# Two routed experts' sums and the gates' pace in an attention, MoE and MoE kernel on one core

## The chip, the cores and the metric

One core of a Trainium2 chip runs the whole program. Its engines are TensorE (PE, matmuls, with PEld for its weight loads), VectorE (DVE), ScalarE (ACT), GpSimd (POOL) and SyncE (SP, which issues the DMAs). Each takes its own instructions in the order in which the program issued them, and waits where a value or a buffer isn't ready. The metric is the device time of one execution in microseconds; lower is better.

## The reference

Three layers follow each other: attention with a threshold on the scores, a gated MLP, and a mixture over all eight experts. Only the last is touched:

```python
logits = x @ w_gate                       # 2304 tokens, 512 wide, 8 experts
P = np.exp(logits - logits.max())
for _ in range(8):                        # 2304 x 8 table made balanced
    P /= P.sum(1, keepdims=True) + 1e-09
    P /= P.sum(0, keepdims=True) + 1e-09
    P *= N / E
for e in range(E):                        # every expert on every token
    h = np.maximum(x @ w1[e], 0.0)        # 512 -> 1024
    out += P[:, e:e + 1] * (h @ w2[e])    # 1024 -> 512
```

## The kernel before

**Number format.** Every fp32 product is three matmuls: each operand is split into a high part (a copy by ACT in a shorter format) and a low part (the rest, one subtraction on POOL or DVE), and high x high, high x low and low x high are added in PSUM (`mm3`, lines 844 to 846, and `up`, lines 1207 to 1209).

**Passes and steps.** The 2304 tokens go through the experts in three passes `u` of 768 tokens, two blocks of 384. A pass has 32 steps: eight experts, four pairs of 128-wide slices of the inner width each (`PAIRS` = 4, `NG` = 32). The steps are numbered `k` = 0 to 95; `g = k % NG` is a step's number in its pass and `g // PAIRS` its expert.

**A step.** `up(k, u)` makes the hidden values of four block-and-slice pairs by seven products in place of eight (sums of weights and of tokens are multiplied and recombined). Each of its seven parts is one `next(products)`; its parts end in a copy on ACT, a sum on DVE, a Relu on ACT and a low part on DVE (`hidden`, lines 1221 to 1228). The sums that line 1221 writes are called `s`, `u` and `av` in the trace, in this order; the last product adds onto the PSUM bank that the sum `u` has read. `mix(k, u)` multiplies the hidden values with `w2`: six items of six matmuls, each 128 tokens by 512, into one of four PSUM banks (`ps_o`, results `y`), and adds the result to `acc` in SBUF. While the gates aren't ready the first expert's result is added with weight one; at `g == PAIRS` (the first step of the second expert) `acc` is scaled by gate 0 (line 1288), and from there on one multiply-add per item (line 1289) brings gate and sum.

**Order.** It is written out by hand. In step `k` the parts of `up(k)` alternate with calls of `between`, each of which issues one item of the mixing of step `k - 1` (B1 to B6 in the text below), up to two parts of the weights' preparation from the queue `w_parts`, and one call of `sink`. A plain step is: two products, B1, product, B2, product, B3, product, B4, two products, B5, B6. The first step of a pass has B1, B2 and B3 behind the first two products.

**Weights.** `a_steps(k + 1)` queues the sums of `w1`'s blocks (DVE, line 1074 and the two after it, and one at line 1081) and their splits into the tiles `wa`, `wb`, `wc` (ACT, then POOL at line 1071). `b_steps(k)`, queued behind the last product of step `k`, splits `w2` into `b{k}h` on ACT and `b{k}l` on POOL (line 1100), which the mixing in step `k + 1` needs.

**Gates.** `gate_steps` is a generator that `sink` holds from the end of step 1 on. Nineteen of its calls do work: three for the maximum and the exponential, then for each of the eight rounds one that makes the row sums, scales, and adds up the columns within a partition (a row call, lines 1177 to 1182), and one that adds up over partitions by a small matmul and scales (a column call, lines 1185 to 1189). Line 1326 drains what is left at the start of step 5.

**Tokens of the next pass.** `x_first` and `x_second` split parts of them (tiles `X{u}_11`, `_21`, `_22`; ACT, then POOL at line 1024). `x_sums` makes four differences on DVE (line 1038) and splits them (`_t1` to `_t4`; ACT, then two low parts on DVE and two on POOL).

**Memory.** `new` takes the oldest of 26 free SBUF slots, `drop` gives one back; a writer of a slot waits for the readers of what was in it.

Of the kernel before, what the change touches and what calls it, by code (L numbers as in the profile page):

```python
# [10 lines left out]
F32 = mybir.dt.float32  # L11
# [4 lines left out]
ALU = mybir.AluOpType  # L16
# [3 lines left out]
P = 128  # L20
# [111 lines left out]
def attention_moe_moe_kernel(  # L132
# [22 lines left out]
    nc = tc.nc  # L155
    B, H, S, D = q.shape
    NT, DM = out.shape
# [9 lines left out]
    NBLK = NT // BLK  # L167
    NTB = BLK // P
# [24 lines left out]
    def copy_act(o, i):  # L193
        nc.scalar.activation(out=o, in_=i, func=AF.Copy)  # L194
# [519 lines left out]
    def new(shape, dt, name):  # L714
        tag = free_slots.popleft()
        t = slots[tag[0]].tile(shape, dt, tag=tag, name=name)
        home[name] = tag
        return t

    def drop(name):  # L720
        free_slots.append(home.pop(name))
# [5 lines left out]
    PAIRS = FE // P // 2  # L727
    NG = E * PAIRS
# [14 lines left out]
    for f in range(NF1):  # L743
        for nm, x in (("g", w_gate), ("v", w_val)):
            t = dram.tile([P, CC, P], F32, tag=f"{nm}{f}", name=f"first_{nm}{f}")
# [96 lines left out]
    def mm3(ps, a, b, start, stop):  # L842

        nc.tensor.matmul(ps, a[0], b[0], start=start, stop=False)  # L844
        nc.tensor.matmul(ps, a[0], b[1], start=False, stop=False)  # L845
        nc.tensor.matmul(ps, a[1], b[0], start=False, stop=stop)  # L846
# [85 lines left out]
    def logits(i):  # L932

        ps = ps_o.tile([P, 512], F32, tag="o", name=f"lg{i}")
        u, second = divmod(i, 2)
        n = E if u else 2 * E
        if u:
            mms = [(gw[:, c], x2[i][:, c, :]) for c in range(CC)]
        else:
            parts = (("11", 0), ("t1", 0), ("22", 2)) if second else (("11", 0), ("21", 2))  # L940
            mms = [
                (gws[:, c0 + c].rearrange("p a e -> p (a e)"), xo[u, nm][x][:, c, :])
                for nm, c0 in parts for c in range(2) for x in range(2)
            ]
        for x, (a, b) in enumerate(mms):
            nc.tensor.matmul(ps[0:n, 0:BLK], a, b, start=(x == 0), stop=(x == len(mms) - 1))
        lg = tmp.tile([2 * E, BLK], F32, tag="lg", name="lg", bufs=2)
        copy_act(lg[0:n], ps[0:n, 0:BLK])
        lgs[i] = lg
# [69 lines left out]
    def x_op(u, nm, x, eng):  # L1019

        t = new([P, 2, 2, BLK], F32R, f"X{u}_{nm}")
        xo[u, nm] = hi, lo = t[:, 0], t[:, 1]
        copy_act(hi, x)
        eng.tensor_tensor(lo, x, hi.bitcast(F32), op=ALU.subtract)

    def x_first(u):

        for nm, c in (("11", 0), ("21", 2)):
            x_op(u, nm, x2[2 * u][:, c:c + 2, :], nc.gpsimd)

    def x_second(u):
        x_op(u, "22", x2[2 * u + 1][:, 2:4, :], nc.gpsimd)

    def x_sums(u):

        (b11, b21), (b12, b22) = ((x[:, 0:2, :], x[:, 2:4, :]) for x in x2[2 * u:2 * u + 2])
        for nm, out, a, b in (("t1", b11, b12, b11), ("t3", b12, b22, b12), ("t2", b22, b22, b11), ("t4", b21, b21, b22)):
            nc.vector.tensor_tensor(out, a, b, op=ALU.subtract)
        for nm, x, eng in (("t2", b22, nc.vector), ("t1", b11, nc.gpsimd), ("t3", b12, nc.vector), ("t4", b21, nc.gpsimd)):
            x_op(u, nm, x, eng)  # L1040
        drop(f"x2_{2 * u}")
        drop(f"x2_{2 * u + 1}")
# [3 lines left out]
    def a_load(k):  # L1046

        e, j = divmod(k % NG, PAIRS)
        f = 2 * j * P
        src = w1[e].rearrange("(c p) f -> p c f", p=P)  # L1050
        t = raws["a", k] = rw.tile([P, 6, 2, P], F32, tag="raw", name=f"a{k}")
        nc.sync.dma_start(t[:, 0:2].rearrange("p a c f -> p (a c) f"), src[:, :, f:f + P])
        nc.sync.dma_start(t[:, 2], src[:, 2:4, f + P:f + 2 * P])
        nc.sync.dma_start(t[:, 3], src[:, 0:2, f + P:f + 2 * P])
# [29 lines left out]
    def a_drop(k):  # L1084
        wa.pop(k)
        for x in "abc":
            drop(f"w{x}{k}")

    def b_load(k):
        e, j = divmod(k % NG, PAIRS)  # L1090
        f = 2 * j * P
        raws["b", k] = [tmp.tile([P, DM], F32, tag="cv", name=f"b{k}_{n}", bufs=2) for n in range(2)]
        for n, t in enumerate(raws["b", k]):
            nc.sync.dma_start(t, w2[e][f + n * P:f + (n + 1) * P, :])
# [62 lines left out]
    gate_p = sm.tile([P, NTILE, E], F32, tag="gate_p", name="gate_p")  # L1157
# [32 lines left out]
                gate_p, gate_p, cs.rearrange("p (o e) -> p o e", o=1).to_broadcast([P, NTILE, E]), op=ALU.mult)  # L1190
            yield

    acc = [None] * NBLK
    hid = {}

    PARTS = {1: ("11", "11"), 2: ("12", "21"), 3: ("s4", "22"), 4: ("22", "t4"), 5: ("s1", "t1"), 6: ("s2", "t2"), 7: ("s3", "t3")}
# [58 lines left out]
    def store(i, n):  # L1255
        t = i * NTB + n
        if t < B * NR:
            b, r = divmod(t, NR)
            dst = out[b * S:b * S + MAIN, :].rearrange("(p r) d -> p r d", r=NR)[:, r, :]
            nc.sync.dma_start(dst, acc[i][:, n, :])  # L1260
        else:
            for x in range(2):
                b = 2 * (t - B * NR) + x
                nc.sync.dma_start(out[b * S + MAIN:(b + 1) * S, :], acc[i][x * TL:(x + 1) * TL, n, :])

    def mix(k, u):

        g = k % NG
        e = g // PAIRS
        wh, wl = wb[k]  # L1270
        for x in range(2 * NTB):
            half, n = divmod(x, NTB)
            i = 2 * u + half
            hs = [hid[k, u, f"{f}{half + 1}"] for f in (1, 2)]
            if g == 0 and n == 0:
                acc[i] = new([P, NTB, DM], F32, f"acc{i}")
            t = ps_o.tile([P, 512], F32, tag="o", name=f"y{k}_{i}_{n}")
            sl = slice(n * P, (n + 1) * P)
            for f, h in enumerate(hs):
                mm3(t, (h[:, 0, sl], h[:, 1, sl]), (wh[:, f], wl[:, f]), f == 0, f == 1)  # L1280
            a = acc[i][:, n, :]
            if g == 0:
                copy_act(a, t)
            elif e == 0:
                nc.vector.tensor_tensor(a, t, a, op=ALU.add)
            else:
                if g == PAIRS:
                    nc.vector.tensor_scalar(a, a, gate_p[:, i * NTB + n, 0:1], None, op0=ALU.mult)
                nc.vector.scalar_tensor_tensor(a, t, gate_p[:, i * NTB + n, e:e + 1], a, op0=ALU.mult, op1=ALU.add)  # L1289
            if g == NG - 1:  # L1290
                store(i, n)
                if n == NTB - 1:
                    drop(f"acc{i}")
            yield

    steps2 = [(k, k // NG) for k in range(3 * NG)]
    sink = None
    w_parts = deque()

    def w_some(n):  # L1300
        for _ in range(n):
            if w_parts:
                w_parts.popleft()()
# [5 lines left out]
    def between(n):  # L1309
        nonlocal sink  # L1310
        x = next(fill, None)
        if callable(x):
            x()
        w_some(n)
        if sink is not None and next(sink, 0) == 0:
            sink = None

    for k, u in steps2:
        if k + 2 < len(steps2):
            a_load(k + 2)  # L1320
        b_load(k)
        products = up(k, u)
        fill = iter([down_last, lambda: logits(4)]) if k == 0 else mix(*steps2[k - 1])
        if k + 1 < len(steps2):
            w_parts.extend(a_steps(k + 1))
        if k == 5:
            while sink is not None:
                between(0)

        first = k and u > steps2[k - 1][1]  # L1330
        next(products)
        next(products)
        between(2)
        if first:
            between(1)
            between(1)
        next(products)
        if not first:
            between(2)
        next(products)  # L1340
        between(2)
        next(products)
        between(2)
        next(products)
        next(products)
        w_parts.extend(b_steps(k))
        a_drop(k)
        if k % NG == NG - 3 and u < 2:
            x_first(u + 1)
            x_second(u + 1)  # L1350
        if k % NG == NG - 1 and u < 2:
            for nm in ("11", "21", "22", "t1", "t2", "t3", "t4"):
                drop(f"X{u}_{nm}")
            x_sums(u + 1)
        between(2)
        between(2)
        w_some(99)
        if k:
            wb.pop(k - 1)
            drop(f"b{k - 1}h")  # L1360
            drop(f"b{k - 1}l")
        if k == 0:
            logits_t(3)
            logits(5)
            logits_t(4)
        if k == 1:
            logits_t(5)
            sink = gate_steps()
    for _ in mix(*steps2[-1]):
        pass  # L1370
# [32 lines left out]
```

## Time and profile before

| | us |
|---|---|
| median of 3 runs | 2386.51 (2383.09 to 2387.18) |
| the profiled execution | 2386.1 |
| its span | 2384.3 |

The profile is one execution; its span starts and ends with the core's own work. The engines' busy times add up side by side. An engine's wait is put down to what released it, and the duration of a line's instruction is long when it stood blocked after it had started. The experts' steps fill the span from about 800 us to its end.

### The profile page before, as it was taken

What the parts mean: (1) busy time and instruction counts of PE and PEld (TensorE: products, weight loads), DVE (VectorE), ACT (ScalarE), POOL (GpSimd) and SP (SyncE); (2) the same over time, 40 slices, a digit from 0 to 9 for tenths busy, and PEclk for the clock granted to TensorE, in tenths of its full rate; (3) what the DMA queues carried; (4) which work ended last, traced back from release to release, by engine and by line L of the source; (5) the groups of instructions that cost most, each with busy time, mean ns of one, the idle gap of its engine ahead of it and who ended that gap; (6) DMA issues with size and microseconds to landing.
All of it is one profiled execution on the core that took longest, in us unless ns stands there. A gap on an engine that the chain in (4) does not pass through costs nothing.

```text
span 2384.3 us, 33858 instructions
## 1 busy us (share of the span) xinstructions
PE 2301.3 (97%) x12353; PEld 2049.6 (86%) x12353; DVE 1656.6 (69%) x2707; ACT 1028.5 (43%) x1889; POOL 1167.0 (49%) x1043
## 2 busy tenths in 40 slices
PE   7999999999999989999999899999999899999999
PEld 5767769999999877999898798899988788989987
DVE  6898977385743377777776667777776577777775
ACT  4777863332223333444444343444444434444442
POOL 4887856454544333444445444444445444444442
PEclk9999999999999999999999999999999999999999
DMA  8666632020100111222222221222222222222221
GB/s 209 149 166 151 143 91 67 16 65 27 54 18 1 36 54 54 71 72 65 66 65 68 78 72 59 70 71 71 66 63 68 80 67 67 63 71 71 71 63 53
DMA packets 203702, 174.71 MB, mean 73 GB/s; under 512 B 52112, under 2 KB 163728, under 8 KB 203536
## 3 DMA queue, kind: packets, MB, share of 16 engines
q1 hardware_dynamic: 203536, 172.56, 26.6%
q8 instruction: 97, 1.59, 0.3%
q14 instruction: 69, 0.57, 0.1%
HBM read 136.07 MB, written 7.08 MB: 60 GB/s over the span
## 4 chain that ended last, share of the span: by engine, by line
PE 82%; POOL 5%; DVE 5%; issue 3%; DMA 2%; SPq 1%; ACT 1%; POOLq 0%; DVEq 0%; ACTq 0%
PE y L845 11%; PE y L846 10%; PE y L844 10%; PE up L1208 9%; PE up L1207 9%; PE up L1209 9%; PE d L846 2%; PE d L845 2%; PE d L844 2%; PE v L844 2%; PE v L846 2%; PE v L845 2%; PE g L844 2%; PE g L846 2%; PE g L845 2%
## 5 line engine op out<-in xcount | busy, mean ns | idle before, releaser
L1289 DVE SCALAR_TENSOR_TENSOR acc<-y,gate_p,acc 128x512 f32<-128x512 f32 x504 | 376.4, 747 | 112.8 <-PE y L846 110.4
L1071 POOL TENSOR_TENSOR wa<-a,wa 128x768 fp32r<-128x768 f32 x96 | 177.4, 1848 | 232.6 <-ACT wa L194 230.5
L1071 POOL TENSOR_TENSOR wb<-a,wb 128x768 fp32r<-128x768 f32 x96 | 177.7, 1851 | 204.7 <-ACT wb L194 201.6
L1208 PE MATMUL up<-X_t,wb 128*128 128x384 f32 x576 | 195.5, 339 | 0.0
L1207 PE MATMUL up<-X_t,wb 128*128 128x384 f32 x576 | 194.3, 337 | 0.0
L1209 PE MATMUL up<-X_t,wb 128*128 128x384 f32 x576 | 193.8, 336 | 0.0
L989 POOL TENSOR_TENSOR h<-av,h 128x384 fp32r<-128x384 f32 x72 | 89.1, 1239 | 198.0 <-ACT h L194 198.0
L1071 POOL TENSOR_TENSOR wc<-a,wc 128x256 fp32r<-128x256 f32 x96 | 77.2, 804 | 191.4 <-ACT wc L194 188.0
L194 ACT ACTIVATE wb<-a 128x768 fp32r<-128x768 f32 x96 | 81.2, 846 | 196.2 <-DVE a L1076 190.7
L1074 DVE TENSOR_TENSOR a<-a 128x256 f32<-128x256 f32 x96 | 155.6, 1620 | 0.0
L1221 DVE TENSOR_TENSOR s<-up,s 128x384 f32<-128x384 f32 x96 | 53.5, 557 | 138.2 <-PE up L1209 137.3
L985 DVE TENSOR_TENSOR av<-v,s 128x384 f32<-128x384 f32 x72 | 40.0, 556 | 153.8 <-PE v L846 137.6
L478 DVE SCALAR_TENSOR_TENSOR em<-ns,st,ee 128x576 f32<-128x576 f32 x144 | 137.3, 954 | 12.3 <-POOL st L465 8.1
L1207 PE MATMUL up<-X,wa 128*128 128x384 f32 x384 | 130.0, 338 | 0.0
L1209 PE MATMUL up<-X,wa 128*128 128x384 f32 x384 | 129.7, 338 | 0.0
L1208 PE MATMUL up<-X,wa 128*128 128x384 f32 x384 | 129.3, 337 | 0.0
L469 ACT ACTIVATE ee<-ns,st 128x576 f32<-128x576 f32 x144 | 111.5, 775 | 35.3 <-DVE ns L461 34.4
L1208 PEld LDWEIGHTS up<-X_t,wb 128*128 128x128 f32 x576 | 109.2, 190 | 13.4
L1207 PEld LDWEIGHTS up<-X_t,wb 128*128 128x128 f32 x576 | 109.2, 190 | 12.5 <-issue 0.6
L454 PE MATMUL s<-kk,qs 128*128 128x288 f32 x512 | 98.5, 322 | 21.1 <-DVE ns L461 11.7
L461 DVE TENSOR_SCALAR_CACHE_REDUCE ns<-s 128x576 f32<-128x576 f32 x144 | 108.4, 752 | 12.6 <-PE s L454 6.3
L194 ACT ACTIVATE u<-up 128x384 f32<-128x384 f32 x96 | 47.3, 492 | 153.8 <-PE up L1209 153.8
(1298 smaller groups left out, 7275.8 us busy)
## 6 DMA issues: line engine op xcount, KB each, us to landing
b<-in_moe_w_dram SPq DMA_DIRECT2D x192, 256.0 KB, 2.7
a<-in_moe_w_dram SPq DMA_DIRECT2D x96, 256.0 KB, 2.9
a<-in_moe_w_dram SPq DMA_DIRECT2D x192, 128.0 KB, 2.9
kk<-khl SPq DMA_DIRECT2D x64, 320.0 KB, 5.0
qs<-qhl SPq DMA_DIRECT2D x64, 128.0 KB, 3.1
raw_g<-in_moe_w_gate_dram SPq DMA_DIRECT2D x6, 768.0 KB, 4.6
raw_v<-in_moe_w_val_dram SPq DMA_DIRECT2D x6, 768.0 KB, 4.6
raw_o<-in_moe_w_out_dram SPq DMA_DIRECT2D x6, 768.0 KB, 4.3
```

Of the source, the lines that this page charges most:

```text
L194: nc.scalar.activation(out=o, in_=i, func=AF.Copy)
L469: nc.scalar.activation(out=ee[t], in_=sc[t], func=AF.Exp, bias=stat[t][:, 0:1], scale=-1.0)
L478: nc.vector.scalar_tensor_tensor(m, sc.pop(t), stat.pop(t)[:, 1:2], ee.pop(t), op0=ALU.is_le, op1=ALU.mult, accum_out=sums[p][:, s:s + 1],)
L844: nc.tensor.matmul(ps, a[0], b[0], start=start, stop=False)
L845: nc.tensor.matmul(ps, a[0], b[1], start=False, stop=False)
L846: nc.tensor.matmul(ps, a[1], b[0], start=False, stop=stop)
L1071: yield lambda: nc.gpsimd.tensor_tensor(lo, x, hi.bitcast(F32), op=ALU.subtract)
L1074: nc.vector.tensor_tensor(s1, a21, a22, op=ALU.add)
L1207: nc.tensor.matmul(ps, ah, bh, start=start and d == 0, stop=False, skip_group_check=True)
L1208: nc.tensor.matmul(ps, ah, bl, start=False, stop=False, skip_group_check=True)
L1209: nc.tensor.matmul(ps, al, bh, start=False, stop=d == 1, skip_group_check=True)
L1289: nc.vector.scalar_tensor_tensor(a, t, gate_p[:, i * NTB + n, e:e + 1], a, op0=ALU.mult, op1=ALU.add)
```

## The change

Three edits. The second expert's sum gets a tile of its own (`second{i}`, two of them) in the first pass: its first step copies the result there on ACT, the next three add, and in the first step of the third expert the first expert's sum is scaled by gate 0 and the second's added with gate 1, by one more multiply-add per item. `between` calls `sink` only every second time, and the drain stands in front of step 9 in place of step 5. The splits of the next pass's tokens move: `x_first` from a pass's third-last step, ahead of the split of `b`, to the end of its fourth-last step; `x_second` to the end of the third-last; and in a pass's last step what is queued in `w_parts`, the split of `b`, is issued ahead of `x_sums` in place of behind it.

```diff
--- before.py
+++ after.py
@@ -1190,7 +1190,7 @@
                 gate_p, gate_p, cs.rearrange("p (o e) -> p o e", o=1).to_broadcast([P, NTILE, E]), op=ALU.mult)
             yield
 
-    acc = [None] * NBLK
+    acc = {}
     hid = {}
 
     PARTS = {1: ("11", "11"), 2: ("12", "21"), 3: ("s4", "22"), 4: ("22", "t4"), 5: ("s1", "t1"), 6: ("s2", "t2"), 7: ("s3", "t3")}
@@ -1283,9 +1283,23 @@
                 copy_act(a, t)
             elif e == 0:
                 nc.vector.tensor_tensor(a, t, a, op=ALU.add)
+            elif e == 1 and u == 0:
+
+                if g == PAIRS and n == 0:
+                    acc["second", i] = new([P, NTB, DM], F32, f"second{i}")
+                a = acc["second", i][:, n, :]
+                if g == PAIRS:
+                    copy_act(a, t)
+                else:
+                    nc.vector.tensor_tensor(a, t, a, op=ALU.add)
             else:
-                if g == PAIRS:
+                if g == PAIRS or u == 0 and g == 2 * PAIRS:
                     nc.vector.tensor_scalar(a, a, gate_p[:, i * NTB + n, 0:1], None, op0=ALU.mult)
+                if u == 0 and g == 2 * PAIRS:
+                    x = acc["second", i][:, n, :]
+                    nc.vector.scalar_tensor_tensor(a, x, gate_p[:, i * NTB + n, 1:2], a, op0=ALU.mult, op1=ALU.add)
+                    if n == NTB - 1:
+                        drop(f"second{i}")
                 nc.vector.scalar_tensor_tensor(a, t, gate_p[:, i * NTB + n, e:e + 1], a, op0=ALU.mult, op1=ALU.add)
             if g == NG - 1:
                 store(i, n)
@@ -1295,6 +1309,7 @@
 
     steps2 = [(k, k // NG) for k in range(3 * NG)]
     sink = None
+    turn = [0]
     w_parts = deque()
 
     def w_some(n):
@@ -1312,7 +1327,8 @@
         if callable(x):
             x()
         w_some(n)
-        if sink is not None and next(sink, 0) == 0:
+        turn[0] += 1
+        if sink is not None and turn[0] % 2 and next(sink, 0) == 0:
             sink = None
 
     for k, u in steps2:
@@ -1323,7 +1339,7 @@
         fill = iter([down_last, lambda: logits(4)]) if k == 0 else mix(*steps2[k - 1])
         if k + 1 < len(steps2):
             w_parts.extend(a_steps(k + 1))
-        if k == 5:
+        if k == 2 * PAIRS + 1:
             while sink is not None:
                 between(0)
 
@@ -1345,16 +1361,18 @@
         next(products)
         w_parts.extend(b_steps(k))
         a_drop(k)
-        if k % NG == NG - 3 and u < 2:
-            x_first(u + 1)
-            x_second(u + 1)
         if k % NG == NG - 1 and u < 2:
             for nm in ("11", "21", "22", "t1", "t2", "t3", "t4"):
                 drop(f"X{u}_{nm}")
+            w_some(99)
             x_sums(u + 1)
         between(2)
         between(2)
         w_some(99)
+        if k % NG == NG - 4 and u < 2:
+            x_first(u + 1)
+        if k % NG == NG - 3 and u < 2:
+            x_second(u + 1)
         if k:
             wb.pop(k - 1)
             drop(f"b{k - 1}h")
```

## Rows read from the trace of the kernel before

**Rows 1.** The page: busy time of each engine, its share, instructions.
```profile
...
PE 2301.3 (97%) x12353; PEld 2049.6 (86%) x12353; DVE 1656.6 (69%) x2707; ACT 1028.5 (43%) x1889; POOL 1167.0 (49%) x1043
```

**Rows 2.** Waits of PE: us in total, times, the longest.
```profile
...
PE cs L1185 <- DVE cs L1182: 10.9, 5, 3.4
...
PE y L845 <- POOL b29l L1100: 4.2, 2, 3.9
...
PE y L844 <- ACT b31h L194: 3.5, 1, 3.5
```

**Rows 3.** Busy time by stretch, and one step's first mixing product.
```profile
...
839.10:1007.10 168.00, 151.98 (x722) 132.87 (x722) 124.66 (x235) 59.51 (x110) 63.41 (x46) 0.96 0.20 57
1007.10:1304.30 297.20, 297.20 (x1485) 267.47 (x1483) 215.69 (x323) 124.98 (x231) 134.12 (x95) 1.00 0.24 68
1304.30:1382.80 78.50, 67.62 (x313) 58.68 (x313) 43.87 (x68) 32.03 (x59) 37.46 (x26) 0.93 0.24 74
...
L844 PE MATMUL y<-b30h,h x12: 387/389/390, 1326.1 to 1338.9; 128*128 128x512 f32 x12
```

**Rows 4.** Busy time in a step with gates, and in a plain one.
```profile
...
857.50:880.70 23.20, 18.34 (x85) 15.94 (x85) 19.07 (x45) 6.36 (x12) 7.30 (x6) 0.93 0.17 47
960.20:975.80 15.60, 15.60 (x79) 14.04 (x79) 11.35 (x17) 6.48 (x12) 7.06 (x5) 1.00 0.26 71
```

**Rows 5.** PE behind a wait for the column sums: granted clock, then instructions.
```profile
...
868.00:872.00 4.00, 2.73 (x9) 0.65 0.00 0
...
869.27 0.60 PE L1185 MATMUL cs<-cs,ones 128*128 128x8 f32 x2 [3.35 <-DVE cs L1182]
869.72 0.67 PE L1207 MATMUL up<-X_t,wb 128*128 128x384 f32 x1
```

**Rows 6.** DVE: one gate line (ns least/median/most), then a row call by time.
```profile
...
L1189 DVE TENSOR_TENSOR gate_p<-gate_p,cs x8: 308/310/1355, 857.0 to 907.7; 128x144 f32<-128x144 f32 x8
...
897.30 0.29 DVE L1177 TENSOR_REDUCE rs<-gate_p 128x18 f32<-128x144 f32 x1
...
898.85 0.55 DVE L1228 SCALAR_TENSOR_TENSOR h<-up,h 128x384 fp32r<-128x384 f32 x1
```

**Rows 7.** DVE: the weights' sum (ns least/median/most), then a plain step by time.
```profile
...
L1074 DVE TENSOR_TENSOR a<-a x96: 415/1773/1844, 797.7 to 2343.4; 128x256 f32<-128x256 f32 x96
...
1012.17 0.75 DVE L1289 SCALAR_TENSOR_TENSOR acc<-y,gate_p,acc 128x512 f32<-128x512 f32 x1
...
1015.33 0.55 DVE L1221 TENSOR_TENSOR u<-up,u 128x384 f32<-128x384 f32 x1
```

**Rows 8.** PE in order of time, the same step.
```profile
...
1007.12 0.39 PE L844 MATMUL y<-b10h,h 128*128 128x512 f32 x1
...
1008.51 0.33 PE L1207 MATMUL up<-X_t,wb 128*128 128x384 f32 x1
...
1016.86 0.33 PE L1207 MATMUL up<-X,wc 128*128 128x384 f32 x1
```

**Rows 9.** Two lines of DVE: ns least/median/most; its waits behind the second.
```profile
...
L1288 DVE TENSOR_SCALAR acc<-acc,gate_p x18: 478/486/1973, 905.8 to 1964.5; 128x512 f32<-128x512 f32 x18
...
L1228 DVE SCALAR_TENSOR_TENSOR h<-s,h x96: 557/558/1744, 803.8 to 2357.9; 128x384 fp32r<-128x384 f32 x96
...
  ACT h L1227: 178.9, 292
```

**Rows 10.** POOL around the first change of pass.
```profile
...
1301.61 5.41 POOL L1024 TENSOR_TENSOR X<-x,X 128x768 fp32r<-128x768 f32 x3 [2.48 <-ACT X L194]
...
1343.43 4.33 POOL L1024 TENSOR_TENSOR X_t<-x,X_t 128x768 fp32r<-128x768 f32 x2 [6.86 <-ACT X_t L194]
```

**Rows 11.** DVE there: the additions of the fifth and sixth item.
```profile
...
1346.03 1.39 DVE L1289 SCALAR_TENSOR_TENSOR acc<-y,gate_p,acc 128x512 f32<-128x512 f32 x2
```

**Rows 12.** ACT there: four token parts, and a copy of a mixing result.
```profile
...
1341.78 3.04 ACT L194 ACTIVATE X_t<-x 128x768 fp32r<-128x768 f32 x4 [3.54 <-DVE x L1038]
...
1368.84 0.60 ACT L194 ACTIVATE acc<-y 128x512 f32<-128x512 f32 x1 [0.54 <-PE y L846]
```

## The prediction

> **What bounds the kernel now.** I read the page first: PE is busy for 97% of the span [rows 1], so only PE's idle time and its slow stretches can be won. The waits of PE come next [rows 2]: of what the diff touches, the column sums of the gate table (`cs`) and, at the two passes' ends, the products that wait for the splits of `b29` and `b31` stand out. A wait's total leaves out the clock and the delays behind it, so I cut the span at the first mixing product of a step and compare stretches [rows 3]. Loop step `k` runs the mixing of weights `b{k-1}`. From `b10` to `b29` nineteen steps take 297.2 us, 15.64 each, with PE never idle: that is what a step costs. Nine steps from `b1` to `b10`, in which the gates are made, take 168.0 in place of 140.8: 27.2 too many. Four steps from `b29` to `b33`, over the first change of pass, take 78.5 in place of 62.6: 15.9 too many. The second change of pass repeats the first. So about 27.2 + 2 x 15.9 = 59 us lie in the places that the diff rewrites.
>
> Why they are lost differs. In a step with gates DVE is busy 19.07 us, in a plain one 11.35 [rows 4]: three gate calls a step bring DVE above the 15.64 of PE, and PE, in order, waits for `cs`, once for 3.35 us, behind which its granted clock is 0.65 for 4 us, a mix of its two levels of 2.4 and 1.2 GHz [rows 5]. At the change of pass DVE is not full; there the splits of the next tokens stand in ACT's and POOL's queues ahead of the split of `b`, which PE needs next. POOL splits three tokens parts from 1301.61 for 5.41 us and only then `b29`; two more from 1343.43 for 4.33, and only then `b31` [rows 10].
>
> **A plain step, for the walk.** Count from its first mixing product, 1007.12 [rows 8]. A mixing item is six matmuls, 1.39 us (1007.12 to 1008.51); so a product of `up` is (15.64 - 6 x 1.39) / 7 = 1.04. With the loop's order, items B1 to B6, the third item ends at 6.26, `up`'s last product begins at 9.74 (1016.86), B5 at 10.78, the next step at 15.64. DVE ends the weights' sums behind B1 at 5.05 and the sum `u` at 1015.33 + 0.55, thus 8.76 [rows 7]. The last product writes on the bank that this sum reads, so DVE may come 1.0 us late there and no more. Mixing results have four banks: an item waits for the addition of the fourth before it.
>
> **Gates in half pace (steps 2 to 8).** One call at B1, B3, B5. Nineteen working calls then end in step 8, B1, and the drain in front of step 5 goes; step 9, which first uses the gates, needs none. A row call costs DVE 898.85 - 897.30 = 1.55 us [rows 6], a column call about 1, so 1.5 of each a step add 3.8, to 15.2: just under a step, if nothing collides. Collisions exist: a 0.31 us multiply has taken 1.36 [rows 6]. By place:
> - row at B1: 5.05 + 1.55 = 6.6, PE asks at 6.26: a wait of 0.4;
> - row at B3: pushes `u` to 8.76 + 1.55 = 10.3 against 9.74: a wait of 0.6;
> - row at B5: PE asks one item, two products and an item later (4.9 us): hidden, with 0.8 us of lag carried on.
> Six steps with one or two of these: 3 us. The small products themselves stay; each holds PE 0.45 (869.27 to 869.72) at the lower clock [rows 5], 0.3 taken at the full one, ten of them 3 us. I put 6 for steps 2 to 8. Bounds: 3 (only the small products) and 12 (each of eight column calls waits 1.1 us more).
>
> **Second expert apart.** At g = 4 six DVE scalings and six multiply-adds become six ACT copies of PSUM, 0.60 each [rows 12]; ACT is busy 6.48 of 15.6 [rows 4], so these 3.6 us are hidden by PE. At g = 5 to 7 an addition replaces a multiply-add, at about the same price. The bill comes in step 9: per item the scaling (0.48 free, up to 1.97), a multiply-add of two SBUF tensors that the trace lacks, and the usual 0.75 [rows 7, 9]. Nearest to the new one is 128x384 from two SBUF tensors, 0.56 free and 1.74 at worst; with the 0.75 of 128x512 out of PSUM I take 0.75 free. DVE's step: 11.35 + 6 x (0.48 + 0.75) = 18.7, 3.1 above PE's. Walked through its queue, B1 to B3 with two blocked operations bring `u` to about 12.4 against 9.74 (2.7 us of wait), and the split of `b9` behind it comes some 2.5 us late. I take 5. Bounds: 2 (later steps' free 4.3 us absorb the rest) and 9 (every item blocked once).
>
> Gates and second expert together: -27.2 + 6 + 5 = -16.2.
>
> **First splits of the next tokens.** `x_first` moves from step 29, ahead of `b29`, to the end of step 28, behind `b28`; `x_second` behind `b29`. POOL is then taken by tokens until about 3.5 us into step 29 and the weights' split starts 2 us later; it is wanted only a step later. The price is DVE's: its weight sums wait for POOL, `u` comes 0.8 us late. I take 1.0 (bounds 0 and 3). The 3.9 us wait for `b29` [rows 2] and its clock go.
>
> **Sums of the next tokens.** In step 31 the split of `b31` now comes first, so B1 of step 32 doesn't wait for it. What is late next is DVE: four subtractions and two splits stand ahead of the additions of B5 and B6, as before (these at 1346.03 [rows 11]). PE, from 1326.1 [rows 3], would reach B1 of step 32 at 1341.76 and B3 at 1344.5. B3 needs B5's bank, free at 1346.7: a wait of 2.2 that the wait for `b31` covers today. POOL's two parts of `b31` now run during the subtractions. A DVE sum that takes 0.42 at the least takes 1.77 in the median, beside POOL's split [rows 7], and the two-tensor operation has taken 1.74 in place of 0.56 [rows 9]: one of the two engines stands still. Two such blocks of 1.2 push the additions by some 2.3, so B3 waits 4.5 in all (0.3 of it already in B1, for the end of `b31`'s split). Add (1 - 0.65) x 4 = 1.4 for the clock behind such a wait [rows 5] and 0.6 for `u`: 6.5. Bounds: 2.5 (no block, no clock) and 10.
>
> The Trainium skill ("SBUF — State Buffer", section "SBUF: two separate sides") says that a DVE operation on two SBUF inputs and a GpSimd operation that reads SBUF exclude each other for the whole instruction. The medians and maxima above agree. By the rule both blocks happen and the sum stays at 6.5; without it the additions would keep their place and it would be 6.5 - 2.3 = 4.2. The rule speaks against putting `b31` ahead here, and against the multiply-add of two SBUF tensors.
>
> Per change of pass: -15.9 + 1.0 + 6.5 = -8.4; two of them -16.8.
>
> **Sum.** -16.2 - 16.8 = -33.0. The profiled execution took 2386.1 us, 1.8 around its span; the median shown is 2386.51, 0.4 above it. 2386.1 - 33.0 = 2353.
>
> **Rivals.**
> - *The pass changes give little.* DVE's blocks come in every one of its six operations, B3 waits 7 or more and the clock falls to half. Each change then saves 3 or less: 2386 - 16 - 6 = 2364. For it: POOL's queue is full there. Against it: ACT delivers the four token parts in one run of 3.04 us [rows 12], so DVE's two splits meet POOL once, as today.
> - *DVE is not late.* The blocks fall into its idle times: gates 3, step 9 2, each pass 3.5: -22 - 25, 2339. For it: a plain step leaves DVE 4.3 us. Against it: 178.9 us over 96 steps, 1.9 a step, are waits for ACT between a sum and its split [rows 9], which can't be used.
> - *The slots run out.* Two more of 26 slots are held in steps 5 to 9. If a new weights tile got a slot that the same step still reads, its split could begin only at the step's end, and POOL's 7.05 us a step [rows 4] would stand open: 5 x 7.05 = 35 us, slower from 4.7 such steps on: 2386.1 - 33 + 35 = 2388 at five, and more with the clock. Against it: followed through the code's order, one slot stays free at the least, and each one taken was given back in the step before or earlier, behind products that are done.
> - *It does not do what it says.* If calls were late, step 9 would drain four, say, at today's price of 27.2 / 19 = 1.4 us each, 6 us: 2359. The count (three calls in each of steps 2 to 7, the last in step 8) excludes it.
>
> **Numbers.** The sum as forecast, 2344 to 2362: 0.62. Pass changes give little: 0.17. DVE not late: 0.15. Calls late: 0.02. Slots: 0.03, a third of it within 0.2%. An unseen neutral case: 0.01. About 0.2% (4.8 us) is what a measurement can tell from no change. Faster 0.96, same 0.02, slower 0.02. Range for 8 in 10: 2338 to 2367, from the bounds of step 9, of B3's wait and of the second rival.
>
> **What would show it.** Right: waits for `cs` almost gone; the nine steps from `b1` to `b10` at about 152; the next waits at `u` in step 9 and at an item of step 32 behind a DVE addition, none for `b29` and `b31`; the new multiply-add at 0.75, some far longer. Wrong: waits of PE for weights in steps 5 to 9 (slots), a wait of 6 us or more in step 32, or DVE's additions ahead of PE throughout.

## The result, and the profile after

The changed kernel takes 2355.09 us (median of 4; 2353.39 to 2357.32) against 2386.85 (median of 4) for the kernel before: ratio 0.9867, 95% interval 0.9854 to 0.9879, 31.8 us less. The forecast was 2353, in a range of 2338 to 2367.

The page of the profiled execution, against [rows 1]: span, then busy time, share and instructions of each engine.

```profile
span 2351.5 us, 33864 instructions
...
PE 2289.1 (97%) x12353; PEld 2041.5 (87%) x12353; DVE 1670.2 (71%) x2707; ACT 1031.1 (44%) x1895; POOL 1174.1 (50%) x1043
```

PE is busy 12.2 us less with the same 12353 matmuls, whose mean granted clock rose from 0.988 to 0.995; the other 20.6 of the span's 32.8 us are idle time. Where they lay is seen in PE's waits, against [rows 2]:

```profile
...
PE y L844 <- DVE acc L1303: 7.6, 2, 3.8
PE up L1207 <- DVE u L1221: 3.6, 4, 2.4
PE cs L1185 <- DVE cs L1182: 2.7, 3, 1.6
...
PE y L845 <- POOL b9l L1100: 1.6, 2, 0.9
```

The waits for `cs` fall from 10.9 to 2.7 us, those for the splits of `b29`, `b31`, `b61` and `b63` are gone. New are a wait of 3.8 us, twice, for an addition of a mixing result, waits of 3.6 us in all for the sum `u`, the longest 2.4, and two short ones for the low part of `b9`.

Stretches, against [rows 3] and [rows 4]: start and end, length, then busy time of PE, PEld, DVE, ACT and POOL with instructions, granted clock, DMA. The first is from `b1` to `b10`, the second its steps 2 to 8, the third and fourth its last two steps (9 and 10), the fifth from `b29` to `b33`.

```profile
...
837.50:992.20 154.70, 147.01 (x723) 129.66 (x722) 126.38 (x235) 62.21 (x116) 64.14 (x46) 0.99 0.22 62
837.50:954.50 117.00, 113.32 (x567) 100.29 (x566) 94.47 (x189) 49.77 (x92) 49.78 (x36) 1.00 0.23 64
954.50:972.90 18.40, 16.02 (x81) 14.10 (x79) 15.66 (x24) 5.68 (x11) 4.80 (x4) 1.00 0.19 54
972.90:992.20 19.30, 17.67 (x79) 15.26 (x78) 16.25 (x23) 6.76 (x14) 9.56 (x7) 0.91 0.19 55
1289.80:1358.80 69.00, 64.97 (x314) 57.02 (x313) 48.43 (x68) 31.91 (x58) 35.91 (x24) 0.98 0.28 84
```

Cut at the first mixing product of a step, and with 15.64 us a plain step:

| stretch | plain | before | after | forecast |
|---|---|---|---|---|
| `b1` to `b8` (steps 2 to 8) | 109.5 | 136.7 | 117.0 | 115.5 |
| `b8` to `b10` (steps 9 and 10) | 31.3 | 31.3 | 37.7 | 36.3 |
| `b1` to `b10` | 140.8 | 168.0 | 154.7 | 151.8 |
| `b28` to `b33`, first change of pass | 78.2 | 94.2 | 85.0 | 85.7 |
| `b60` to `b65`, second change of pass | 78.2 | 94.7 | 86.1 | 85.7 |

The three stretches save 13.3 + 9.2 + 8.6 = 31.1 us of the span's 32.8. The rest, 1.6, lies ahead of the first mixing product (823.0 before, 821.4 after), which the change does not touch; over all runs of this study that point falls between 821 and 829. So a time of one run is read to some 4 us. Stretches of the same code mostly agree to a few tenths between runs, and some only to about 1 us: the second change of pass, 86.1 here, takes 85.0 to 85.2 in four other runs with the same code there, and `b1` to `b10` takes 168.0 in the kernel before and 167.0 in `tokens_only`.

**Step 9.** DVE in order of time, from its first item:

```profile
...
956.95 2.21 DVE L1300 SCALAR_TENSOR_TENSOR acc<-second,gate_p,acc 128x512 f32<-128x512 f32 x1
...
961.58 0.75 DVE L1300 SCALAR_TENSOR_TENSOR acc<-second,gate_p,acc 128x512 f32<-128x512 f32 x1
...
966.22 0.55 DVE L1221 TENSOR_TENSOR u<-up,u 128x384 f32<-128x384 f32 x1
```

The new operation, written `acc<-second`, takes 0.75 us, as taken from its neighbours, and 2.21 when POOL's split of weights has started just before. `u` ends at 966.77, and PE stands for it, and in the next step for the low part of `b9`:

```profile
...
966.82 0.44 PE L1207 MATMUL up<-X,wc 128*128 128x384 f32 x1 [2.38 <-DVE u L1221]
...
974.16 0.50 PE L845 MATMUL y<-b9l,h 128*128 128x512 f32 x1 [0.90 <-POOL b9l L1100]
```

**Change of pass.** DVE in step 31, the last three of four differences and the additions of B5 and B6:

```profile
...
1319.06 1.93 DVE L1038 TENSOR_TENSOR x<-x 128x768 f32<-128x768 f32 x1
1321.02 2.93 DVE L1038 TENSOR_TENSOR x<-x,x 128x768 f32<-128x768 f32 x2
...
1327.30 1.40 DVE L1303 SCALAR_TENSOR_TENSOR acc<-y,gate_p,acc 128x512 f32<-128x512 f32 x2
```

POOL beside it, the two low parts of `b31`:

```profile
...
1318.16 3.98 POOL L1100 TENSOR_TENSOR b31l<-b,b31h 128x512 fp32r<-128x512 f32 x2 [2.26 <-ACT b31h L194]
```

PE at its third item of step 32, and the granted clock (the number behind the instructions) of the four microseconds around its end:

```profile
...
1328.09 0.79 PE L844 MATMUL y<-b31h,h 128*128 128x512 f32 x1 [3.79 <-DVE acc L1303]
```

```profile
...
1328.00:1332.00 4.00, 3.91 (x13) 0.62 0.04 15
```

In the kernel before POOL was idle beside the differences [rows 10]. There DVE's four differences, and POOL's two low parts of `b30` with no difference beside them:

```profile
...
1338.75 0.95 DVE L1038 TENSOR_TENSOR x<-x,x 128x768 f32<-128x768 f32 x1
1339.74 0.96 DVE L1038 TENSOR_TENSOR x<-x 128x768 f32<-128x768 f32 x1
1340.73 1.95 DVE L1038 TENSOR_TENSOR x<-x,x 128x768 f32<-128x768 f32 x2
...
1323.20 2.55 POOL L1100 TENSOR_TENSOR b30l<-b,b30h 128x512 fp32r<-128x512 f32 x2 [2.42 <-ACT b30h L194]
```

The differences took 0.95 to 0.98 each; here it is 1.93 for the second and 2.93 for the last two, and POOL's two parts took 3.98 in place of 2.55. By these times two of the differences stood still for about 1 us each, and POOL's two parts for 1.4 us between them: the two engines took turns. The additions stand 21.9 us behind the step's first mixing product (1305.4), in place of 19.9 before ([rows 3, 11]), and PE waits 3.79 us for them where it waited for `b31` before.

### The profile page after: what moved, and what is told of

Same layout as the page of the kernel before. It is cut to its first block, busy times and chain, and to the rows that moved or that the text cites. A ratio compares the mean times of both kernels' runs of the same rounds, so it can differ in the third digit from the quotient of the medians.

```text
span 2351.5 us, 33864 instructions
## 1 busy us (share of the span) xinstructions
PE 2289.1 (97%) x12353; PEld 2041.5 (87%) x12353; DVE 1670.2 (71%) x2707; ACT 1031.1 (44%) x1895; POOL 1174.1 (50%) x1043
## 4 chain that ended last, share of the span: by engine, by line
PE 82%; DVE 6%; POOL 5%; issue 3%; DMA 2%; ACT 1%; SPq 1%; POOLq 0%; DVEq 0%; ACTq 0%
PE y L845 10%; PE y L846 10%; PE y L844 10%; PE up L1207 9%; PE up L1208 9%; PE up L1209 9%; PE d L845 2%; PE d L846 2%; PE d L844 2%; PE v L844 2%; PE v L845 2%; PE v L846 2%; PE g L844 2%; PE g L845 2%; PE g L846 2%
## 5 line engine op out<-in xcount | busy, mean ns | idle before, releaser
L1303 DVE SCALAR_TENSOR_TENSOR acc<-y,gate_p,acc 128x512 f32<-128x512 f32 x480 | 357.6, 747 | 78.8 <-PE y L846 76.8
L1221 DVE TENSOR_TENSOR s<-up,s 128x384 f32<-128x384 f32 x96 | 53.4, 556 | 132.8 <-PE up L1209 132.8
L1208 PEld LDWEIGHTS up<-X_t,wb 128*128 128x128 f32 x576 | 109.1, 189 | 13.3
L454 PE MATMUL s<-kk,qs 128*128 128x288 f32 x512 | 98.1, 320 | 20.3 <-DVE ns L461 10.9
L454 PEld LDWEIGHTS s<-kk,qs 128*128 128x128 f32 x512 | 73.5, 193 | 41.0 <-DVE ns L461 16.3
```

What stands on the lines that cost most here:

```text
L454: nc.tensor.matmul(ps[:, n, 0:HS], lhs, rhs[:, ko + n * HS:ko + (n + 1) * HS], start=(x == 0), stop=(x == len(ops) - 1))
L1208: nc.tensor.matmul(ps, ah, bl, start=False, stop=False, skip_group_check=True)
```

## The experiments

Each is an edit to the changed kernel unless said otherwise. Lines behind the edit of `early_diffs` have numbers 7 higher in it, in `all_three` and in `late_wb`.

### Only the gates: `gates_only`

The tokens' splits go back to their old places.

```diff
+        if k % NG == NG - 3 and u < 2:
+            x_first(u + 1)
+            x_second(u + 1)
         if k % NG == NG - 1 and u < 2:
...
-            w_some(99)
             x_sums(u + 1)
...
-        if k % NG == NG - 4 and u < 2:
-            x_first(u + 1)
-        if k % NG == NG - 3 and u < 2:
-            x_second(u + 1)
```

> The changed kernel with the tokens' splits back in their old places: only the half pace and the second expert's own sum are left. The theory (two parts that pay apart, each in its own stretch) expects the stretch from b1 to b10 at 154.7 us as in the changed kernel, the four steps from b29 to b33 back at 78.5, and 2355.1 + 9.2 + 8.6 = 2373 us, 13 to 14 below the kernel before. The rival, that the second sum's two slots or the shifted queues also matter at the changes of pass, expects one of these two stretches to differ by more than 1 us from its value there. The rival that the gain is all in the tokens' splits expects 2386.

2372.34 us (4 runs; ratio 0.9931, 0.9914 to 0.9948): 17.2 less than the kernel before beside it, 2389.54, and 14.5 less than its 2386.85 beside the changed kernel. `b1` to `b10` 154.7, `b29` to `b33` 77.7, `b28` to `b33` 93.3. PE's waits:

```profile
...
PE y L845 <- POOL b29l L1100: 3.9, 1, 3.9
PE y L844 <- ACT b31h L194: 3.5, 1, 3.5
...
PE cs L1185 <- DVE cs L1182: 2.7, 3, 1.5
```

The stretches are where the theory put them, to 0.8 us. The first rival is out; the one that gives the tokens all the gain too.

### Only the tokens: `tokens_only`

The kernel before, with `x_first`, `x_second` and the split of `b31` moved as in the change.

> The kernel before with only the tokens' splits moved. The theory expects the stretch from b1 to b10 at 168.0 us as before, the waits for the low parts of b29, b31, b61 and b63 gone, one wait of 3.8 us at the third item of steps 32 and 64 behind a DVE addition, and 2386.9 - 17.8 = 2369 us. With the other half's 13 to 14 us the two gains add up to the whole. The rival that the two parts depend on each other expects the two gains to miss the whole of 31.8 us by more than 3.

2367.72 us (4 runs; ratio 0.9911, 0.9896 to 0.9926), 21.8 less than 2389.54. `b1` to `b10` 167.0, `b28` to `b33` 85.0. PE's waits:

```profile
...
PE cs L1185 <- DVE cs L1182: 10.1, 5, 3.4
PE y L844 <- DVE acc L1289: 7.6, 2, 3.8
```

By the times beside them the two gains are 17.2 + 21.8 = 39.0, 7 more than the whole, which would be the rival's case; but the kernel before was 2.7 us slower in this set. Against 2386.85 they are 14.5 + 19.1 = 33.6, 1.8 over the whole. The stretches decide, free of it: 13.3 us go in the one kernel, 9.2 + 9.5 in the other, where they went in the whole. The stretches that an edit leaves as they were differ from the kernel before by 0.2 to 1.0 us. To about 1 us the two parts are independent.

### The pace: `full_pace`

```diff
-        if sink is not None and turn[0] % 2 and next(sink, 0) == 0:
+        if sink is not None and next(sink, 0) == 0:
```

> The changed kernel with one gate call at every item again, the second expert still apart. The theory (three calls a step fill DVE beyond a step) expects steps 2 to 4 to be as long as before, 18.4, 23.2 and 20.9 us, waits for the column sums of 8 to 11 us, step 5 some 17 in place of 24.7, steps 9 and 10 as in the changed kernel, and in all about 9 us more than it, 2364. The rival, that the old cost was the drain in front of step 5 and the items behind it and that the pace is nothing, expects steps 2 to 4 near 16.5 us each and 2355.

2366.13 us, one run. Steps 2 to 5 take 18.4, 21.7, 21.8 and 17.6, `b1` to `b10` 164.0: 9.3 more than the changed kernel. Two of PE's waits, in steps 3 and 4:

```profile
...
872.28 0.39 PE L1185 MATMUL cs<-cs,ones 128*128 128x8 f32 x2 [1.75 <-DVE cs L1182]
...
894.00 0.39 PE L1185 MATMUL cs<-cs,ones 128*128 128x8 f32 x2 [3.33 <-DVE cs L1182]
```

So 9.3 of the 13.3 us are due to the pace. The second expert's own sum, which makes room for it, takes away the drain and the wait behind it (step 5: 24.7 to 17.6) and pays for it in steps 9 and 10 (37.6 in this run too).

### Where the calls stand: `even_calls`

```diff
-        if sink is not None and turn[0] % 2 and next(sink, 0) == 0:
+        if sink is not None and turn[0] % 2 == 0 and next(sink, 0) == 0:
```

> The changed kernel with the gate calls at the second, fourth and sixth item of a step in place of the first, third and fifth; their number and pace stay. The walk by place says that a row call behind the first item is late for PE because the weights' sums stand ahead of it on DVE, and behind the third because the sum u stands behind it. At the even items neither is so: the waits for column sums (2.7 us) and of 0.2 to 0.8 for u in steps 4 and 6 go, and steps 2 to 8 lose 4 us in place of 7.5: stretch b1 to b10 151, time 2351.5. The rival, that DVE is simply full in these steps wherever the calls stand, expects 154.7 and 2355.

2361.7 us, one run (its first mixing product came 7.2 us later than in the changed kernel's profile, so the time tells nothing here). Steps 2 to 8 take 118.6 us in place of 117.0. PE's waits:

```profile
...
PE up L1207 <- DVE u L1221: 5.6, 5, 2.4
...
PE cs L1185 <- DVE cs L1182: 0.5, 1, 0.5
...
PE y L845 <- POOL b4l L1100: 0.3, 1, 0.3
PE y L845 <- POOL b6l L1100: 0.3, 1, 0.3
```

The waits for `cs` fall from 2.7 to 0.5, and others take their place: `u`, 5.6 in place of 3.6, and the low parts of `b`. My reading by place fell; the rival's forecast holds, for the one other place that was tried: DVE is late there too. That it is late because it is full is argued, not shown. In steps 2 to 8 of the changed kernel DVE is busy 94.5 of the 117.0 us, 13.5 a step; only with the 1.9 us a step in which it waits for ACT between a sum and its split [rows 9] does that come to 15.4, near the 15.64 of a plain step.

### Step 9 relieved: `spread_merge`

```diff
                 if g == PAIRS or u == 0 and g == 2 * PAIRS:
-                    nc.vector.tensor_scalar(a, a, gate_p[:, i * NTB + n, 0:1], None, op0=ALU.mult)
-                if u == 0 and g == 2 * PAIRS:
+                    nc.scalar.activation(out=a, in_=a, func=AF.Copy, scale=gate_p[:, i * NTB + n, 0:1])
+                if u == 0 and g == 2 * PAIRS + half:
```

> The changed kernel with the scaling by gate 0 on ACT in place of DVE, in all passes, and the adding of the second expert's sum for a pass's second block one step later: DVE then has 11.35 + 3 x 0.75 = 13.6 us in steps 9 and 10. The theory (step 9 costs 6.4 us because DVE has 18.7 us of work in it) expects steps 9 and 10 at 16.2 us each and the steps 37, 38, 69 and 70, now 16.0 and 16.8, at 15.7: 2355 - 5.3 - 2.5 = 2347. The rival, that the blocking of the two-tensor operation by POOL is the cost and not DVE's load, expects steps 9 and 10 to lose 4 us or more still, 2351 to 2353.

2348.31 us, one run. Steps 9, 10 and 11 by window (columns as above):

```profile
...
957.20:974.10 16.90, 15.92 (x80) 14.03 (x78) 13.79 (x20) 9.77 (x18) 5.79 (x5) 1.00 0.19 60
974.10:990.20 16.10, 15.89 (x79) 13.99 (x78) 12.22 (x19) 6.54 (x13) 7.44 (x5) 1.00 0.23 66
990.20:1006.80 16.60, 15.89 (x79) 13.96 (x79) 12.60 (x19) 6.47 (x12) 8.79 (x7) 1.00 0.24 66
```

They take 49.6 us in place of 53.4, and steps 37, 38, 69 and 70, 16.0 and 16.8 before, 15.6 to 15.7: 3.8 + 3.0 = 6.8 us less, 7.8 expected. Steps 9 and 10 were put right (33.0, 32.4 expected); step 11, with 16.6, was overlooked. Most of step 9's price, 3.8 of 6.5 us, went with the work that was taken off DVE or moved. The time that the new operation stands blocked beyond its 0.75 us went on, 1.74 us over its six instances in place of 2.35, so the rival is not the main cause. The edit does not part load from blocking wholly: three of the six scalings had stood blocked too (1.22, 0.97 and 0.64 us in place of 0.48), and they left DVE with the rest.

### The additions ahead: `sums_behind`

```diff
             w_some(99)
-            x_sums(u + 1)
         between(2)
         between(2)
+        if k % NG == NG - 1 and u < 2:
+            x_sums(u + 1)
```

> The changed kernel with the differences and splits of the next pass's tokens issued behind the last two items of steps 31 and 63. If the 3.8 us wait at the third item of the next step is for the additions that queue on DVE behind these differences, it goes; the walk through the queues then finds the next wait at the product that uses the first token difference, behind ACT's copy, about 2 us, and 1 us at the sum u: some 3 us in all in place of 6.8, 2355 - 7 = 2348. If the wait is for anything else that comes late there (the splits themselves, the low part of b31), it stays at 3.8 or grows, and the time is 2355 or more.

2352.04 us, one run. The wait for the addition is gone, in both changes of pass, so it was for the additions behind the differences. DVE now, B5's addition and the first difference:

```profile
...
1319.04 0.74 DVE L1303 SCALAR_TENSOR_TENSOR acc<-y,gate_p,acc 128x512 f32<-128x512 f32 x1
...
1320.78 1.71 DVE L1038 TENSOR_TENSOR x<-x,x 128x768 f32<-128x768 f32 x1
```

But two waits took its place, PE in step 32 and shortly after:

```profile
...
1328.04 0.44 PE L1207 MATMUL up<-X_t,wb 128*128 128x384 f32 x1 [1.74 <-ACT s L194]
...
1335.07 0.44 PE L1207 MATMUL up<-X_t,wb 128*128 128x384 f32 x1 [1.72 <-ACT av L194]
```

The first, 1.74 for ACT's copy `s`, was foreseen with 2; the second, two products later, was not. `b28` to `b33` falls from 85.0 to 84.3 only, not to 81.

### The differences earlier: `early_diffs`

```diff
-    def x_sums(u):
+    def x_diffs(u):
...
-            nc.vector.tensor_tensor(out, a, b, op=ALU.subtract)
+            yield lambda out=out, a=a, b=b: nc.vector.tensor_tensor(out, a, b, op=ALU.subtract)
+
+    def x_sums(u):
...
+        for fn in diffs[u]:
+            fn()
...
+    diffs = {u: x_diffs(u) for u in range(3)}
...
-        if k % NG == NG - 4 and u < 2:
+        if k % NG == NG - 5 and u < 2:
             x_first(u + 1)
-        if k % NG == NG - 3 and u < 2:
+        if k % NG == NG - 4 and u < 2:
             x_second(u + 1)
+        if NG - 4 <= k % NG < NG - 1 and u < 2:
+            next(diffs[u + 1])()
```

> The changed kernel with the tokens' first splits a step earlier and the four differences spread: one at the end of each of the three steps before a pass's last, one in it. If the change of pass now costs what stands on DVE ahead of the additions, and the two blocks by POOL among it, then DVE has one difference and two splits there in place of four and two, the additions come some 4 us sooner than the third item of the next step needs at most, and the wait of 3.8 us and its clock go: 1.5 us per change in place of 6.8 and 7.9, 2355 - 11.7 = 2343. The rival from the run with the sums behind, that the splits themselves on ACT and POOL are what is late next, expects 4 to 6 us per change still, 2351.

2347.46 us, one run. `b28` to `b33` takes 81.7, the second change 81.6: 3.3 and 4.5 us less than the changed kernel, not 5.3 and 6.4; against the 85.0 to 85.2 that the second change takes in other runs, the 4.5 are 3.5. The 3.8 us wait is gone; what is left is one of 1.83:

```profile
...
1332.76 0.44 PE L1214 MATMUL up<-X_t,wb 128*128 128x384 f32 x1 [1.83 <-ACT av L194]
```

It is for ACT's copy `av`, and ACT has ahead of it the split of `wb`, which had waited 3.67 us for DVE's sums of weights:

```profile
...
1331.49 0.84 ACT L194 ACTIVATE wb<-a 128x768 fp32r<-128x768 f32 x1 [3.67 <-DVE a L1083]
1332.24 0.47 ACT L194 ACTIVATE av<-up 128x384 f32<-128x384 f32 x1
```

### Together, and the next wait pulled: `all_three` and `late_wb`

`all_three` has the edits of `early_diffs`, `spread_merge` and `even_calls`.

> The three edits of the other runs together. If they lie in different stretches and each does what its theory says, the savings add up: 3.5 + 7.8 + 11.7 = 23 us less than the changed kernel, 2332. With the rivals right throughout, 2351 to 2355.

2344.82 us (4 runs; ratio 0.9824, 0.9807 to 0.9840), 10.3 less than the changed kernel, not 23. The edit of `even_calls` cost 1.5 us (steps 2 to 8 take 118.5 in place of 117.0); in the stretches of the others the savings are those that they gave alone.

`late_wb` goes back to the odd calls and moves one split:

```diff
         if first:
             between(1)
-            between(1)
+            between(0)
```

> The three edits together, but with the gate calls at the odd items again (the even ones saved nothing) and, in the first step of a pass, the split of the weights' second part issued behind the product whose result ACT copies, in place of ahead of it. In the run with early differences PE waits 1.83 us for that copy, which stands on ACT behind this split, and the split behind DVE's sums of weights. If that is all that is late there, the wait goes, steps 32 and 64 fall from 18.1 to about 16.3 us, and the time is 2344.8 - 2 x 1.8 - 1.6 = 2340. The rival, that DVE's lateness only shows at the next wait (the sum u, or a bank behind an addition), expects 18 us still and 2343.

2342.04 us (5 runs; ratio 0.9813, 0.9799 to 0.9826). Step 32 falls from 18.2 to 16.3 us, and step 33 rises from 15.9 to 19.0; at the second change 18.1 to 16.4, and 15.9 to 17.4. PE at the start of step 33:

```profile
...
1335.55 0.50 PE L844 MATMUL y<-b32h,h 128*128 128x512 f32 x1 [0.19 <-ACT b32h L194]
1336.90 0.50 PE L845 MATMUL y<-b32l,h 128*128 128x512 f32 x1 [0.85 <-POOL b32l L1107]
...
1338.14 0.50 PE L845 MATMUL y<-b32l,h 128*128 128x512 f32 x1 [0.26 <-POOL b32l L1107]
...
1338.99 0.52 PE L1215 MATMUL up<-X_t,wb 128*128 128x384 f32 x1
```

The wait for the copy goes, and the split of `b32` is late in its place. The changes of pass are no shorter than in `all_three` (82.9 and 81.6 against 81.7 and 81.6). The median is 2.8 us lower. Between the two profiles, 3.2 us apart, 1.6 are gained between `b1` and `b10`, where the odd calls are back, and 2.7 ahead of the first mixing product, untouched by the edit; 1.2 are lost at the first change of pass. So the split moved gave nothing. The rival was right that the lateness shows at the next wait, and wrong in the place: it kept step 32 at 18 us and named `u` or a bank, and it was step 33 and the split of `b32`. Still, this is the fastest version run, 44.5 us below the kernel before.

## Why the prediction was right, point by point

**What a plain step costs, and where the time lay.** 15.64 us held in every run, and 31.1 of the 32.8 us came out of the three stretches named.

**Gates in half pace.** 6 us were put for steps 2 to 8, half of them for the small products and half for waits; they cost 117.0 - 109.5 = 7.5. PE is idle for 117.0 - 113.3 = 3.7 of these, and busy for 3.8 more than in seven plain steps. `full_pace` shows that the pace is what pays. Of the waits named by place, a column call at B3 behind a row call at B1 waited 0.3 to 1.6 (0.4 said) and `u` 0.2 to 0.8 (0.6 said); but `even_calls` moved nearly all of them without a gain, so the places do not explain the cost. The other line, DVE's work at 15.2 us a step, was too high: it is busy 13.5. Why it is late at either place stays open.

**Second expert apart.** ACT's copies hid, as said; the new operation takes 0.75 us, as said. Step 9's wait for `u` was put at 2.7 and is 2.4; the late `b9` at some 2.5, and it shows as two waits of 1.6 in all. So the waits, 4.0, were less than put. But PE is also busy 16.02 + 17.67 = 33.7 us in steps 9 and 10, 2.4 more than in two plain steps, with a granted clock of 0.91 in step 10: the sum for step 9 had no term for the clock behind its waits, though the sum for the change of pass had one. Steps 9 and 10 cost 6.4 us in place of 5. `spread_merge` shows that most of it hung on DVE's load: with part of the work taken off and part moved, steps 9 to 11 stand 49.6 - 46.9 = 2.7 us above three plain steps in place of 53.4 - 46.9 = 6.5.

**First splits.** Put at 1.0 us, they cost 0.4 and 0.6 (steps 29 and 61 take 16.0 and 16.2). The waits for `b29` and `b61` went.

**Sums of the next tokens.** The place of the next wait, B3 of step 32 behind the additions, was right, and `sums_behind` shows that it was for these. 4.5 us of wait were put, 3.8 measured: the additions came 1.95 us later by POOL's blocks, not 2.3. The clock behind it was 0.62 for 4 us, 1.5 us; 1.4 were put. With all that hangs on it the sums cost 69.0 - 62.6 = 6.4 us at the first change and 7.3 at the second, in place of 6.5. The Trainium skill ("SBUF — State Buffer", section "SBUF: two separate sides") says that of a DVE operation on two SBUF inputs and a GpSimd operation that reads SBUF, the one that starts first keeps the other out for its whole length. The trace agrees: the differences' 0.96 became 1.93 beside POOL, and POOL's 2.55 became 3.98. What the blocks cost was not taken apart by a run of its own; the times of the instructions show it.

**The rivals.** The pass changes gave more than little. DVE was late. No product waited for weights in steps 5 to 9, so the slots did not run out. The calls ended in time.

The mis-sized terms are the gate steps and step 9, 1.5 and 1.4 us too low, the second for want of a clock term. The changes of pass gave 1.0 us more than put, and 1.6 came from ahead of the stretches, outside the change; these cancel the first two to 0.3 in the profiled execution (span 32.8 us less, 33.0 put). The mechanisms were right; that the sum came out so close is in part luck.

## What to carry to other kernels

When a wait is taken away, walk the queue of the engine that fed it and name what is late next, with its price: here that found the 3.8 us behind the additions, and twice more a wait that moved rather than went (`sums_behind`, `late_wb`). When an engine is late, another place for its work in the same steps can just move the wait (`even_calls`); what helped here was to take work off it, onto an engine with room (`spread_merge`) or into steps with room (`early_diffs`). Price the clock behind every wait that you foresee, not only behind the longest. Where two parts of a change lie in different stretches, cut the span by stretch: the sums there agree to about 1 us and mostly to tenths, when the times of single runs do not agree to 4 us.

## What the runs showed of the hardware

PE's granted clock fell behind some short waits and not behind others. In `late_wb` waits of 0.19, 0.85 and 0.26 us at the start of step 33 were followed by matmuls of 0.52 us in place of 0.34, and a granted clock of 0.84 and then 0.73 over 4 us each, a mix of its two levels of 1.2 and 2.4 GHz; in the changed kernel a single wait of 1.55 us for `cs` (at 895.33) left it at 1.00. The length of a wait does not decide it alone: PE waits for `u` in step 9 for 2.38 us in the changed kernel and for 2.39 in `even_calls`. The granted clock behind these waits (the number behind the instructions), in this order:

```profile
...
967.00:971.00 4.00, 4.00 (x20) 1.00 0.31 91
...
976.00:980.00 4.00, 4.00 (x14) 0.59 0.34 101
```

What does decide was not tried.
